# Attention ordered by whole pairs of heads in a fused attention and feed-forward kernel

## Chip, cores and metric

The kernel runs on one core of one Trainium2 chip. The metric is the device time of one execution in microseconds (us); smaller is better.

## What is computed

Two blocks follow each other. The attention has 4 batches, 8 heads, 768 positions and head size 64; its mask lets a query see only those keys whose six hashed sign bits equal its own. The feed-forward takes the 3072 rows of 512 values that the attention leaves.

```python
q_bits = (np.einsum('bhsd,dk->bhsk', q, proj) > 0)
k_bits = (np.einsum('bhsd,dk->bhsk', k, proj) > 0)
mask = q_bucket[:, :, :, None] == k_bucket[:, :, None, :]
scores = np.where(mask, scale * np.matmul(q, k.transpose(0, 1, 3, 2)), -1e9)
attn = np.exp(scores - np.max(scores, axis=-1, keepdims=True))
attn = attn / (np.sum(attn, axis=-1, keepdims=True) + 1e-09)
x = np.matmul(attn, v)             # then (B,H,S,D) -> (B*S, H*D)
h = x @ w_in                       # 512 -> 2048
sp = np.maximum(h, 0.0) + np.log1p(np.exp(-np.abs(h)))
out = (h * erf(sp)) @ w_out        # 2048 -> 512
```

## The kernel before

**Work of the attention.** Two heads are handled together as a pair, one on partitions 0 to 63 and one on 64 to 127; there are 16 pairs. A pair has two halves of 384 queries and, in each, two groups of three key chunks, so 4 groups n = 4i to 4i+3 of three blocks (n, c), 12 blocks. For a block TensorE computes scores of 128 keys by 384 queries for both heads (`score`, L548): first a bf16 product of the sign bits (`both`), which puts keys of another bucket far below zero, and onto it the float32 product of k and q. ScalarE takes the exponential into a block of `e_all` (`exponential`, L566). TensorE multiplies six blocks by v (`weigh`, L629, two groups per half) into `av`; ScalarE copies it out (`leave`, L688).

**Divisors.** VectorE adds the six blocks of a half (`sum_keys`, L617); TensorE sums over partitions with a matrix of ones (`divisor`, L664); ScalarE copies that out (`keep_divisor`, L677). Then the divisors go through DRAM to be spread over partitions: `spread`, `gather`, `invert`, `ungather`, `widen` (L707 to L742). `normalise` (L750) applies them and `send` stores x.

**Bits.** `bits_of` (L817) forms the projections of a later pair, ScalarE takes the sign (`sign_of`, L826), VectorE weighs them, and they go through DRAM into `both` by two steps on POOL's queue, `leave_bits` (L846) and `place_bits` (L855).

**Rooms.** Scores and bits share three double banks of PSUM (tag "big"); `av` has one bank, and z_ps takes the bank of `misc`. `e_all` is a ring of nine blocks. `x_sum` and `blocks[1]`, which the feed-forward uses later, hold the sums of the keys meanwhile.

**Weights.** Beside the attention 32 pieces of w_in and w_out are brought in as raw 64-bit numbers (`fetch_weights`, L454, on POOL's queue from the third on) and turned into float32: ScalarE `square_high` (L468) and `keep_normal` (L475), VectorE `move_bits`, `mask_bits`, `add_rest` (L482 to L530). `measure` (L649) takes sums of squares of q and k on ScalarE. `presum_weights` (L771) prepares sums and differences of blocks of w_in in `w_sum`, `presum_x` (L340) those of x; the feed-forward uses seven products P1 to P7 where the plain way needs eight, and likewise M1 to M7 for w_out.

**Order.** TensorE's order in the attention is written out by hand in the list `order`: score groups 2h+1 and 2h+2, at odd h the bits of a later pair, the divisor of the half before, and the two `weigh` of half h. All other engines follow a planner, `arrange`: each operation has an engine, an estimated cost, a rank, a list of what it comes after, and `late`, the time until others see its result; the planner always takes the operation that can start first, by rank among equals. What it emits is a fixed order per engine and per DMA queue; on the chip each engine then works through its own. The feed-forward is planned separately, so all of an engine's attention work stands ahead of its feed-forward work. The last pair's divisor is emitted in the feed-forward through `late`, as are its inversion and normalising.

## Time and profile before

| | us |
|---|---|
| median of 3 runs | 910.3 (910.22 to 911.51) |
| profiled execution | 910.96 |
| its span | 909.2 |
| feed-forward's first matmul starts | 321.51 |

The engines by stage, from the busy times of stretches of the trace (us, and the share of the 16 DMA engines):

| stretch | length | TensorE | VectorE | ScalarE | DMA |
|---|---|---|---|---|---|
| 50 to 89 | 39 | 37.63 | 35.44 | 30.68 | 0.59 |
| 128 to 167 | 39 | 39.00 | 37.43 | 31.65 | 0.64 |
| 245 to 284 | 39 | 39.00 | 36.96 | 31.64 | 0.60 |
| 321 to 360 | 39 | 39.00 | 30.60 | 27.13 | 0.31 |
| 360 to 900 | 540 | 540.00 | 347.28 | 290.62 | 0.19 |

In the profile a line such as L548 is a line of the kernel; "out<-in" are its tiles; "128*64" after a matmul's tiles is the part of the array that it uses, rows by columns. A float32 matmul shows as two records, and records of matmuls overlap, since they are pipelined. An idle time is followed by what ended it. PE is TensorE, PEld its loading of weights, DVE VectorE, ACT ScalarE, POOL GpSimd, SP SyncE.

### The profile page before, as it was taken

Reading aid. Unit: us, or ns where it says so; the run is one execution under the profiler, and the core shown is the slowest. Engines: PE = TensorE matmul, PEld = TensorE weight load, DVE = VectorE, ACT = ScalarE, POOL = GpSimd, SP = SyncE. Lnnn points to the kernel's source line nnn. Section 1 sums busy time; section 2 is a strip of 40 time slices with the busy share of each in tenths; the row PEclk is TensorE's granted clock in tenths of the full one; section 3 lists DMA queues with packets and bytes.
Section 4 is the critical chain, followed back from the end, with each engine's and each line's share of the span. In section 5 each row is a group of like instructions: output and inputs, shape, how many; then the busy total and the mean of one; then the engine's idle time right before and its main releaser. Section 6 shows DMA issues by size and latency. Waiting matters only on the chain.

```text
span 909.2 us, 12885 instructions
## 1 busy us (share of the span) xinstructions
PE 900.3 (99%) x5016; PEld 661.9 (73%) x5016; DVE 673.3 (74%) x863; ACT 571.9 (63%) x824; POOL 58.2 (6%) x95
## 2 busy tenths in 40 slices
PE   9999999999999999999999999999999999999997
PEld 5444444444444478888888888888888888888886
DVE  5989999989999969986566556756776556655653
ACT  6878887888887849755555545555655555545520
POOL 0211111111121000000000001000100000000000
PEclk9999999999999999999999999999999999999999
DMA  8455677656574231111122114211321023101321
GB/s 203 130 162 148 169 176 189 187 141 165 157 194 136 59 123 64 38 45 70 52 65 82 35 47 105 81 36 47 87 99 35 35 58 94 35 32 52 69 70 50
DMA packets 65013, 86.83 MB, mean 96 GB/s; under 512 B 34348, under 2 KB 47500, under 8 KB 64944
## 3 DMA queue, kind: packets, MB, share of 16 engines
q1 hardware_dynamic: 56384, 63.81, 24.6%
q0 software_dynamic: 8112, 21.66, 8.6%
q8 instruction: 41, 0.67, 0.3%
q10 hardware_dynamic: 448, 0.46, 0.2%
q14 instruction: 28, 0.23, 0.1%
HBM read 64.67 MB, written 17.30 MB: 90 GB/s over the span
## 4 chain that ended last, share of the span: by engine, by line
PE 92%; issue 1%; DMA 1%; ACT 0%; POOL 0%; DVE 0%; DVEq 0%; ACTq 0%; POOLq 0%
PE M L1317 32%; PE X L1204 28%; PE st L548 14%; PE av L629 12%; PE M L1204 3%; PE z_ps L664 1%; PE bits L817 1%; DMA raw<-in_w_in_dram 0%; POOL both L855 0%; ACT e_all L566 0%; ACT keep L468 0%; DMA bd<-sg 0%; DVE u L1352 0%; ACT x L688 0%; DVEq L1727 0%
## 5 line engine op out<-in xcount | busy, mean ns | idle before, releaser
L1244 DVE SCALAR_TENSOR_TENSOR e<-w,e 128x1024 f32<-128x1024 f32 x144 | 173.8, 1221 | 8.9 <-ACT w L1238 4.2
L566 ACT ACTIVATE e_all<-st 128x768 f32<-128x768 f32 x192 | 150.9, 813 | 11.9 <-PE st L548 11.5
L1238 ACT ACTIVATE w<-h,cq 128x1024 f32<-128x1024 f32 x144 | 155.6, 1137 | 0.2 <-DVE e L1244 0.2
L548 PE MATMUL st<-q,k 64*128 64x384 f32 x768 | 155.0, 483 | 0.0
L1226 DVE TENSOR_TENSOR h<-X,h 128x512 f32<-128x512 f32 x65 | 44.8, 689 | 146.0 <-PE X L1204 145.8
L1317 PE MATMUL M<-w_out_sb,h 128*128 128x256 f32 x576 | 141.5, 379 | 0.0
L629 PE MATMUL av<-e_all,v 128*64 128x385 f32 (+1 forms) x768 | 131.1, 490 | 0.0
L1204 PE MATMUL X<-x,w_in_sb 128*128 128x256 f32 x512 | 121.0, 379 | 0.0
L1317 PEld LDWEIGHTS M<-w_out_sb,h 128*128 128x128 f32 x576 | 109.4, 190 | 14.9
L1222 ACT COPY h<-X 128x512 f32<-128x512 f32 x85 | 49.3, 580 | 112.4 <-PE X L1204 112.3
L1234 ACT ACTIVATE e<-h,cq 128x1024 f32<-128x1024 f32 x48 | 55.2, 1150 | 82.7 <-DVE h L1226 82.7
L1204 PEld LDWEIGHTS X<-x,w_in_sb 128*128 128x128 f32 x512 | 97.3, 190 | 13.2
L629 PEld LDWEIGHTS av<-e_all,v 128*64 128x64 f32 x768 | 52.4, 136 | 67.2 <-issue 65.2
L1317 PE MATMUL M<-wt,S 128*128 128x256 f32 x384 | 95.6, 379 | 0.0
L548 PEld LDWEIGHTS st<-q,k 64*128 64x128 f32 x768 | 68.2, 188 | 34.9 <-issue 34.2
L1204 PE MATMUL X<-x_sum,w_sum 128*128 128x256 f32 x344 | 81.3, 379 | 0.0
L1317 PEld LDWEIGHTS M<-wt,S 128*128 128x128 f32 x384 | 73.0, 190 | 9.9
L1204 PEld LDWEIGHTS X<-x_sum,w_sum 128*128 128x128 f32 x344 | 65.4, 190 | 8.9
L548 PE MATMUL st<-both 64*128 64x384 bf16 x384 | 62.9, 324 | 1.6 <-ACT e_all L566 1.4
L1259 DVE TENSOR_TENSOR h<-h,e 128x1024 f32<-128x1024 f32 x48 | 58.0, 1221 | 3.7 <-ACT e L1255 3.6
L1255 ACT ACTIVATE e<-e 128x1024 f32<-128x1024 f32 x48 | 50.4, 1054 | 7.8 <-DVE e L1244 7.4
L548 PEld LDWEIGHTS <-both 64*128 64x128 bf16 x384 | 19.5, 94 | 43.1 <-issue 21.2
(126 smaller groups left out, 1073.4 us busy)
## 6 DMA issues: line engine op xcount, KB each, us to landing
wt<-wt SPq DMA_DIRECT2D x24, 768.0 KB, 4.2
raw<-in_w_out_dram POOLq DMA_DIRECT2D x16, 512.0 KB, 4.6
raw<-in_w_in_dram POOLq DMA_DIRECT2D x14, 512.0 KB, 4.3
v<-in_v_dram SPq DMA_DIRECT2D x32, 192.0 KB, 4.8
xs<-x SPq DMA_DIRECT2D x16, 384.0 KB, 3.1
q<-in_qkT_dram SPq DMA_DIRECT2D x30, 192.0 KB, 4.2
k<-in_qkT_dram SPq DMA_DIRECT2D x30, 192.0 KB, 4.4
r<-rd SPq DMA_DIRECT2D x30, 192.0 KB, 3.4
```

What stands on the lines that cost most here:

```text
L548: nc.tensor.matmul(out=st[:, ab, 0:HS], lhsT=d["k" + src][rows, keys], rhs=d["q" + src][rows, cols], start=(part == 0), stop=(part == 1),)
L566: nc.scalar.activation(out=e[:, :, 0:HS], in_=st[:, :, 0:HS], func=AF.Exp, scale=scale)
L629: nc.tensor.matmul(out=d["av"][rows, 0:w], lhsT=d["v"][:, g * GC + c, rows], rhs=e[:, ab, 0:w], start=(g == 0 and c == 0), stop=(g == 1 an ...
L1204: nc.tensor.matmul(out=d[where][:, u, :], lhsT=a[:, kc, f : f + P], rhs=b[:, kc, :], start=(first and u == 0 and kc == 0), stop=(last and ...
L1222: nc.scalar.copy(out=quarter(p, q), in_=st[p][where])
L1226: nc.vector.tensor_tensor(out=h, in0=st[p][where], in1=h, op=ALU.add)
L1234: nc.scalar.activation(out=s, in_=unit(p, v), func=AF.Sigmoid, bias=cq[:, n : n + 1])
L1238: nc.scalar.activation(out=q, in_=unit(p, v), func=AF.Sigmoid, scale=GATE_S[j][0], bias=cq[:, j : j + 1])
L1244: nc.vector.scalar_tensor_tensor(out=s, in0=st[p].pop(("q", v, j)), scalar=GATE_S[j][2], in1=s, op0=ALU.add, op1=ALU.mult,)
L1255: nc.scalar.activation(out=s, in_=s, func=AF.Tanh, scale=GATE_LEAD)
L1259: nc.vector.tensor_tensor(out=h, in0=h, in1=st[p].pop(("s", v)), op=ALU.mult)
L1317: nc.tensor.matmul(out=banks[name][:, sub, :], lhsT=a[:, u, sub * P : (sub + 1) * P], rhs=b[:, u, :], start=(c == 0 and k == 0), stop=(c = ...
```

## The change

- TensorE's order is by whole pairs: the 12 score blocks of a pair, then `weigh` of all four groups (24 products with v, one for each block and head, which are 48 records in the profile), then the bits of pair i+2 and the divisor of pair i-1. Pair 0 has bits 1 ahead of its products with v, and the last pair has the divisor there.
- One divisor step covers both halves of a pair. It writes into the second bank of the double bank that holds the bits, so the two share one of the three slots of the scores, which is free when both have been copied out.
- The halves' products with v have two banks: the old one and that of `misc`.
- Each half of a pair has six blocks of its own for its exponentials: `e_even`, and `e_odd`, which lies in the room of `w_sum`. `area` holds w_sum, blocks[0], x_sum and blocks[1] in this order. The last half of all uses tiles of the load pool.
- The sums of keys are formed with five wide additions per pair, in two rooms that alternate by pair.
- As `w_sum` is occupied, `presum_weights` 0 to 3 run in the last pair and 4 to 7 in the feed-forward (`late` 3 to 6, ahead of the third product's P5, P6, P7 and P3). Loading the first tile of x and preparing it come later too.
- There are three rooms for raw pieces instead of two, and two each for `keep` and `top`; a piece is asked for every 1.9 groups instead of 2.

```diff
-    w_sum = const.tile([P, 3, 2, FH], F32, name="w_sum")
+    AW, AX_, AB = 6 * FH, 6 * TH, NK * T
+    area = const.tile([P, AW + AX_ + 2 * AB], F32, name="area")
+    w_sum = area[:, 0:AW].rearrange("p (n k c) -> p n k c", n=3, k=2)
+    x_last = const.tile([P, HS], F32, name="x_last")
...
-    x_sum = const.tile([P, 3, 2, TH], F32, name="x_sum")
-    for n in range(2):
-        blocks.append(const.tile([P, NK, T], F32, name=f"x{n}"))
+    x_sum = area[:, AW + AB : AW + AB + AX_].rearrange("p (n k c) -> p n k c", n=3, k=2)
+    for at in (AW, AW + AB + AX_):
+        blocks.append(area[:, at : at + AB].rearrange("p (k t) -> p k t", k=NK))
...
-            tc.tile_pool(name="rawp", bufs=2) as rawp,
+            tc.tile_pool(name="rawp", bufs=3) as rawp,
...
-            NE = 3 * GC
-            e_all = ep.tile([P, NE, 2, HS + 1], F32, name="e_all")
-            nc.vector.memset(e_all[:, :, :, HS : HS + 1], 1.0)
+            NE = 2 * GC
+            e_even = ep.tile([P, NE, 2, HS + 1], F32, name="e_even")
+            nc.vector.memset(e_even[:, :, :, HS : HS + 1], 1.0)
+            e_odd = area[:, 0 : NE * S].rearrange("p (n a c) -> p n a c", n=NE, a=2)
+            e_last = {}
...
-                for t in (x_sum[:, :, :, :], blocks[1][:, :, :].rearrange("p k (a t) -> p k a t", a=2))
+                area[:, at : at + 4 * S].rearrange("p (h n a c) -> p h n a c", h=2, n=2, a=2)
+                for at in (AW + AB, NE * S)
             ]
+            last_sums = blocks[1][:, :, :].rearrange("p k t -> p (k t)")[:, 0 : 2 * S].rearrange(
...
-                keep = cvt.tile([P, WP], I32, name="keep", tag="keep")
+                keep = cvt.tile([P, WP], I32, name="keep", tag="keep", bufs=2)
...
-                return e_all[:, (n * GC + c) % NE, :, :]
+                if n == NS - 2 or n == NS - 1:
+                    what, m = "qkv"[c], n - (NS - 2)
+                    if (m, c) not in e_last:
+                        shape = [P, NC, P] if what == "v" else [P, S]
+                        room = load.tile(shape, F32, name=what, tag=what)
+                        if what == "v":
+                            room = room.rearrange("p c d -> p (c d)")
+                        e_last[m, c] = room[:, 0:S].rearrange("p (a c) -> p a c", a=2)
+                    return e_last[m, c]
+                return (e_odd if n // 2 % 2 else e_even)[:, n % 2 * GC + c, :, :]
...
+            def sum_steps(i):
+                n = 4 * i
+                if i < NPAIR - 1:
                     return [
-                        ((0, 1, 2, 3), (0, 2), (2, 2), 2),
-                        ((4, 5), "s2", (4, 2), 2),
-                        ((), "s0", "s1", 0),
+                        ((0, 0, 4), (0, 1, 2, 3)),
+                        ((0, 4, 2), (4, 5)),
+                        ((1, 0, 4), (6, 7, 8, 9)),
+                        ((1, 4, 2), (10, 11)),
+                        (None, ()),
                     ]
                 return [
-                    ((0, 1, 3, 4), (0, 2), (3, 2), 2),
-                    ((2,), "s0", (2, 1), 0),
-                    ((5,), "s1", (5, 1), 1),
-                    ((), "s0", "s1", 0),
-                ]
-            def last_sum(h):
-                return len(sum_steps(h)) - 1 if h >= 0 else 0
-            def sum_keys(h, k):
-                i, half = divmod(h, 2)
+                    ((0, 0, 4), (0, 1, 2, 3)),
+                    ((0, 4, 2), (4, 5)),
+                    ((0, 6, 0), ()),
+                ] + [((1, k, 1), (6, 7) if k == 1 else (6 + k,)) for k in range(1, 6)]
...
-                    d["av"] = psum_v.tile([P, 512], F32, name="av", tag="av")
+                    d["av", half] = bank("av") if half else psum_v.tile([P, 512], F32, name="av", tag="av")
...
+                if i == NPAIR - 1:
+                    z = bank("z_ps")[:, 0:HS]
+                else:
+                    room = pairs[i + 3]["bits"] if i + 3 < NPAIR else big("z_ps")
+                    z = room[:, 1, 0:HS]
+                d["z_ps"] = z
+                for half in range(2):
+                    for n in range(4):
+                        ab, part = divmod(n, 2)
+                        nc.tensor.matmul(
+                            out=z[n * QR : (n + 1) * QR, half * HS // 2 : (half + 1) * HS // 2],
+                            lhsT=ones[:, 0:QR],
+                            rhs=d["sum"][:, half, ab, part * HS // 2 : (part + 1) * HS // 2],
+                            start=True,
+                            stop=True,
+                        )
...
+            def keep_divisor(i):
                 d = pairs[i]
-                if half == 0:
-                    d["z"] = home(i, "z")
-                nc.scalar.copy(
-                    out=d["z"][:, half * HS // 2 : (half + 1) * HS // 2], in_=d.pop("z_ps")
-                )
+                d["z"] = home(i, "z")
+                nc.scalar.copy(out=d["z"], in_=d.pop("z_ps"))
...
-            order = [("score", 0)]
-            for h in range(NH):
-                order += [("score", n) for n in (2 * h + 1, 2 * h + 2) if n < NS]
-                if h == 0:
+            order = []
+            PACE = 19
+            for i in range(NPAIR):
+                order += [("score", 4 * i + k) for k in range(4)]
+                if i == 0:
                     order.append(("bits", 1))
-                if h % 2 and (h + 3) // 2 < NPAIR:
-                    order.append(("bits", (h + 3) // 2))
-                if h >= 1:
-                    order.append(("divisor", h - 1))
-                order += [("weigh", 2 * h), ("weigh", 2 * h + 1)]
+                if i == NPAIR - 1:
+                    order.append(("divisor", i - 1))
+                order += [("weigh", 4 * i + k) for k in range(4)]
+                if i + 2 < NPAIR:
+                    order.append(("bits", i + 2))
+                if 0 < i < NPAIR - 1:
+                    order.append(("divisor", i - 1))
             slots = []
             for what, n in order:
+                free = slots[-3] if len(slots) >= 3 else ()
                 if what == "score":
                     i = n // 4
                     after = (("double_first",) if i == 1 else ("place_bits", i),)
                     for c in range(GC):
-                        free = (slots[-3],) if len(slots) >= 3 else ()
+                        free = slots[-3] if len(slots) >= 3 else ()
                         pe(score, (n, c), 0.82 if n or c == 2 else 0.17, after + free)
-                        slots.append(("exponential", n, c))
+                        slots.append((("exponential", n, c),))
                 elif what == "bits":
-                    pe(bits_of, (n,), 0.92 if n > 1 else 1.44, (("start_pair", n), slots[-3]))
-                    slots.append(("sign_of", n) if n > 1 else ("place_first",))
+                    pe(bits_of, (n,), 0.80 if n > 1 else 1.44, (("start_pair", n),) + free)
+                    slots.append((("sign_of", n),) if n > 1 else (("place_first",),))
                 elif what == "divisor":
-                    pe(divisor, (n,), 0.42, (("sum_keys", n, last_sum(n)), ("keep_divisor", n - 1)))
+                    if n + 3 < NPAIR:
+                        free = ()
+                        slots[-1] += (("keep_divisor", n),)
+                    else:
+                        slots.append((("keep_divisor", n),))
+                    pe(divisor, (n,), 0.72, (("sum_keys", n, last_sum(n)),) + free)
                 else:
                     h = n // 2
                     after = (("exponential", n, GC - 1),)
                     if n % 2 == 0:
-                        after += (("leave", h - 1), ("leave_plain", (h - 1) // 2))
-                    pe(weigh, (n,), 2.02, after)
+                        after += (("leave", h - 2), ("leave_plain", (h - 2) // 2))
+                    pe(weigh, (n,), 2.0, after)
...
+                    after = (("score", n, c), ("weigh", n - 4)) + sums_after.get((n - 4, c), ())
+                    if n >= NS - 2:
+                        after += tuple(
+                            ("measure", i, m, half)
+                            for i in (NPAIR - 3, NPAIR - 2)
+                            for m in range(2)
+                            for half in range(2)
+                        )
+                    op(exponential, (n, c), "ACT", 0.735, (0, n, c), after)
...
-                    (("start_pair", 1), ("fetch_weights", n - 1), ("add_rest", n - 2), ("exponential", max(2 * n - 2, 0), 1)),
+                    (("start_pair", 1), ("fetch_weights", n - 1), ("add_rest", n - 3), ("exponential", max(PACE * n // 10 - 2, 0), 1)),
...
-                op(square_high, (n,), "ACT", 0.68, (1, n, 0), (fetched, ("mask_bits", n - 1)))
+                op(square_high, (n,), "ACT", 0.68, (1, n, 0), (fetched, ("mask_bits", n - 2)))
...
-            for k in range(8):
+            for k in range(4):
...
+                        ("weigh", NS - 5),
+                        ("sum_keys", NPAIR - 2, last_sum(NPAIR - 2)),
+                    )
+                    + ((("sum_keys", NPAIR - 1, 2),) if k % 4 == 3 else ()),
+                )
+            op(load_x, (0,), "SP", 1.1, (1, 0), (("send", JP - 1), ("divisor", NPAIR - 3)), late=4.0)
             for k in range(4):
-                op(presum_x, (0, k), "DVE", 0.62, (2, 31, 8 + k), (("load_x", 0), ("presum_x", 0, k - 1), ("divisor", NH - 3)))
+                op(presum_x, (0, k), "DVE", 0.62, (2, 31, 8 + k), (("load_x", 0), ("presum_x", 0, k - 1), ("divisor", NPAIR - 2)))
...
+            else:
+                presum_weights(k + 1)
...
+                for k in range(3, 7):
+                    op(("late", k), "DVE", 1.2, (2, 1, -7 + k), late, (k,), after=(("late", k - 1),) if k > 3 else ())
+                for each in ops:
+                    if each.name in (("P5", 2), ("P6", 2), ("P7", 2), ("P3", 2)):
+                        each.after += (("late", 6),)
```

Not shown: renamed arguments, the planner's estimated costs, ranks and dependencies of the sums, and the last pair's x, which is kept, normalised and sent in two halves.

## The prediction

> **What bounds the kernel now.** The page's first part comes first: who is busy, and in how much of the span.
>
> ```profile
> PE 900.3 (99%) x5016; PEld 661.9 (73%) x5016; DVE 673.3 (74%) x863; ACT 571.9 (63%) x824; POOL 58.2 (6%) x95
> ```
>
> TensorE works in all but 9 us of 909.2. So the stage that is changed can gain from less TensorE time per pair, or from a stall that goes; it loses where a new wait reaches TensorE. The second view is TensorE's own waits up to 400 us:
>
> ```profile
> PE st L548 <- ACT e_all L566: 1.4, 1, 1.4
> PE warm L779 <- DVE ones L247: 1.0, 1, 1.0
> PE st L548 <- ACT both L384: 0.3, 1, 0.3
> ```
>
> Two of these lie in the start-up. The 1.4 us is one event at 62.3 us, looked at below. As nothing else is idle, I read the third view, TensorE's timeline over one pair (two half-pairs), start and length in front:
>
> ```profile
> 158.91 0.34 PE L548 MATMUL st<-both 64*128 64x384 bf16 x2
> 159.08 0.81 PE L548 MATMUL st<-q,k 64*128 64x384 f32 x4
> ...
> 162.96 0.33 PE L548 MATMUL st<-both 64*128 64x384 bf16 x2
> 163.12 0.81 PE L548 MATMUL st<-q,k 64*128 64x384 f32 x4
> 163.86 0.52 PE L817 MATMUL bits<-q,proj_q 128*32 128x384 f32 x2
> ...
> 164.53 0.51 PE L664 MATMUL z_ps<-x_sum,ones 128*32 128x192 f32 x8
> 164.97 4.09 PE L629 MATMUL av<-e_all,v 128*64 128x384 f32 x24
> 168.99 0.34 PE L548 MATMUL st<-both 64*128 64x384 bf16 x2
> ...
> 173.94 0.53 PE L664 MATMUL z_ps<-x,ones 128*32 128x192 f32 x8
> 174.40 4.10 PE L629 MATMUL av<-e_all,v 128*64 128x385 f32 x24
> 178.44 0.34 PE L548 MATMUL st<-both 64*128 64x384 bf16 x2
> ```
>
> The lengths overlap, so I use starts. A pair takes 178.44 - 158.91 = 19.53 us. A score block takes (163.12 - 159.08)/5 = 0.808 us: three passes of two row tiles, one in bf16 (0.16) and one float32 product that counts as two (0.323 each, (0.808 - 0.16)/2).
>
> Six blocks are 4.85 us, but bits begin 4.95 us after the first: 0.10 us is lost where the score run ends. The 24 records of products with v are 12 passes of two column tiles, 12 x 0.323 = 3.88 us; the next run begins after 4.02 to 4.04: 0.15 lost. A divisor is two passes of 192 columns, 2 x 0.162 = 0.32 us, and v's products begin after 0.44 to 0.46: 0.125 lost. Bits to divisor is 0.67 us, two passes of 0.323 and 0.02 lost. So each hand-over between kinds of matmul costs 0.10 to 0.15 us, except between two of one shape.
>
> **What the Trainium skill says.** "TensorEngine Tiling (Array Packing)", Key Properties: a change of the tiling mode, not just of the tile, drains the engine. The trace agrees: the losses are where 64*128, 128*32 and 128*64 meet, and bits to divisor, both 128*32, is nearly free. "TensorE: Matmul & The Clock Gate", Back-to-back issue gap: N/2.4 + 2.5 ns, 162 ns for 384 columns; the bf16 pass (0.16) and half a float32 product (0.323/2) agree. The same page's table of specifications calls the other engines' queues strictly first in, first out; the 1.4 us stall is such a case. "DMA: Bandwidth & Descriptors", Issuing engines are not separate DMA queues: transfers of all issuers interleave on the same 16 engines; below, a small one took 6.4 us beside loads.
>
> **The change, part by part.**
>
> Order on TensorE (the main gain). Run ends before: 32 score runs (0.10), 32 runs of products with v (0.15), 31 divisors (0.125): 3.2 + 4.8 + 3.9 = 11.9 us. After: 16, 16, and 16 ends of slots with a divisor or bits (pair 0 has bits alone, pairs 1 to 14 one slot, pair 15 a divisor): 1.6 + 2.4 + 2.0 = 6.0. The streams are the same: 192 score blocks, 768 records with v, 15 products for bits. Gain 5.9 us, about 0.39 per whole pair (19.14). Against it: the divisor left for the feed-forward stage is now a whole pair's, four passes instead of two, +0.32. Net -5.6. Two hand-overs are not in the trace: products with v to bits, and divisor to scores, some 14 each. At least nothing (bits 128*64 to v at the start followed at the stream's pitch, 16.15 to 16.47), at most twice the dearest seen, 0.3: against the 0.15 and 0.125 that I take this is -3.9 to +4.5 us if both went to the same end; I keep +-2 for the range, since all switches seen lie within 0.05 of each other.
>
> Bits and divisor in one PSUM slot. Scores use three slots; the third block of a pair now waits for the slot that sign_of and keep_divisor must empty. From the last product with v (T): bits from T+0.15, divisor T+0.82 to T+1.47, first block T+1.6, third T+3.2. ACT: leave 0.48, sign 0.46, then the copy, now 384 wide, 0.48 (the leave's row): done near T+2.2. Spare 1.0 us. Nothing; if one measure (0.64) stands before them, still nothing. The second av bank only loosens.
>
> Runs of 12 against ScalarE. After the stall ACT did four exponentials in 2.92 us, so saturated pitch is (2.92 - 0.81)/3 = 0.703, against 0.808 for a block: it gains 0.105 per block. A squaring or a piece's first step put into a run costs it 0.50 to 0.57 (163.07 to 163.57; 152.82 to 153.39), and before TensorE waits it may be late by 0.58 (first exponential ends 160.75, fourth block starts 161.33). One such op fits, a second after five or six blocks. ACT's sum per pair: 12 x 0.703, two leaves 0.96, sign 0.46, copy 0.48, four measures 2.56, 2.1 pieces at 1.38: 15.8 of 19.1 us. So nothing.
>
> VectorE. Five wide steps of 1.79 (165.37 to 167.16) are 8.95 per pair against about 9.1; pieces at 2.1 per pair instead of 2 add 0.38; four preparations of W_in (4.9 us) leave the stage. It stays at 96% (37.43 of 39 us), but what waits for it has more room: a block is overwritten 19 us after its exponential instead of 14. Nothing.
>
> The end of the stage. In the last pair's 19 us VectorE has three wide and five narrow sums (9.3), four preparations (4.9), the four of x (2.75) and a normalise (1.0): about 18. The first to be missed is P6, 3.5 us into the feed-forward (325.07 before), which needs the x sums; I put these some 5 us before it. The other four preparations, 4.9 us, fall between 324 and 342, where VectorE idled 7 us; they are due at the third product (343.4). Nothing; without that cover, up to 3 us. Loading x later: one whole pair remains for 4 us of transfer. Nothing. The two sends and two normalises of pair 15: a late transfer, needed a tile later.
>
> The stall at 62.3 us. POOL's, ACT's and TensorE's timelines there:
>
> ```profile
> 48.72 0.55 POOL L846 DMA_DIRECT2D bd<-sg  x1 [5.14 <-DVE sg L836]
> 55.77 1.15 POOL L855 DMA_DIRECT2D both<-bd  x2 [6.50 <-issue]
> 56.91 1.14 POOL L454 DMA_DIRECT2D raw<-in_w_in_dram  x2
> ```
>
> ```profile
> 61.11 0.69 ACT L468 ACTIVATE keep<-raw 128x512 f32<-128x512 f32 x1 [4.75 <-DMA raw<-in_w_in_dram]
> 61.83 0.72 ACT L475 ACTIVATE keep<-keep,tiny 128x512 int32<-128x512 f32 x1
> 62.46 0.46 ACT L688 COPY x<-av 128x384 f32<-128x384 f32 x1
> 62.82 2.92 ACT L566 ACTIVATE e_all<-st 128x768 f32<-128x768 f32 x4
> ```
>
> ```profile
> 63.68 0.34 PE L548 MATMUL st<-both 64*128 64x384 bf16 x2 [1.37 <-ACT e_all L566]
> ```
>
> The bits' transfer took 6.4 us because the next pair's q, k, v (issued 47.24 to 50.37) were in flight; the fetch of a raw piece was queued on POOL behind the placing of the bits; the piece landed at 61.03; ACT's squaring waited in order, and leave and exponentials behind it. With three raw rooms and two keep and top rooms a fetch may be asked for earlier, so this event should go (-1.37). But bits now fall right at the pair's end, where the next load becomes free to start: the same meeting can come in any pair. Each costs up to 1.4. I take 1.1 for them, under one event; bounds 0 and 14 events.
>
> Sum, on the profiled execution (910.96; span 909.2 and 1.8 around it): -5.6 - 1.4 + 1.1 = -5.9, 905.1. The median of the runs is 0.66 below that execution: 904.4.
>
> **The rivals.**
>
> Slower: the bits' traffic delays the pieces in nearly every pair. Place: POOL's queue, then ACT's squaring in front of exponentials. Price 1.4 per pair; the gain of 7.0 is gone from five events on, and 13 of them give 910.3 - 7.0 + 18 = 921; nine, which I take for its time, 916. For it: loads and bits start together. Against: only one of 14 placings did this before; a fetch has a median landing of 4.3 to 4.6 us and 7.0 are planned.
>
> ScalarE in the runs of 12: a third op in a run, or one that carries lateness over, costs 0.5 in each of 14 pairs: +7, 910. For it: spare of 0.58 against 0.57. Against: the pitch, and that ops are put in only when ACT has caught up.
>
> Dear hand-overs: the two new ones cost 0.25 each, +3, 907.5. For it: never seen. Against: every drain seen.
>
> **How the numbers follow.** Forecast 0.70, 904.4, own range 902 to 907.5 (hand-overs +-2, no stall or two). Dear hand-overs 0.06, ScalarE 0.09, slower rival 0.15. The range leaves out the slower rival and a little of the others: 901.8 to 909.8. A measurement of this kernel tells 0.2% (1.8 us) from no change. Faster, below 908.5: 0.70 + 0.06 + a bit of ScalarE's, 0.77; within, 0.07; slower, above 912.1, 0.16.
>
> **What would show it.** Right: a pair on TensorE's timeline of 19.1 to 19.2 us; scores 12 x 0.808; 48 records with v, then bits, divisor, scores with 0.10 to 0.15 at each change; the feed-forward beginning near 315 instead of 321.5, and as long as before. Wrong: waits of TensorE for exponentials in several pairs, with ACT idle for a raw piece before them (slower rival) or without idle time (ScalarE's); a gap at P6 or at the third product (preparations late); a pair near 19.5 without waits (hand-overs).

## The result, and the profile after

The changed kernel takes 916.05 us (median of 5 runs, 914.37 to 916.87) against 910.8 us (910.22 to 911.94) for the kernel before on the same chip: a ratio of 1.0053 (of the means, as all ratios here), 95% interval 1.0039 to 1.0068. It is slower by about 5 us, where 6 us less had been forecast. The profiled execution is 916.7 us, its span 914.9.

The page's line of busy times for the changed kernel:

```profile
PE 897.7 (98%) x5016; PEld 673.0 (74%) x5016; DVE 668.7 (73%) x837; ACT 562.9 (62%) x808; POOL 58.2 (6%) x95
```

TensorE is busy 2.6 us less than before, yet it is now idle for 17 us of its span instead of 9. What it waited for up to 420 us (total, times, longest, in us):

```profile
PE M L1241 <- DVE h L1263: 5.3, 1, 5.3
PE M L1241 <- ACT h L1259: 2.1, 1, 2.1
PE st L554 <- ACT z L691: 1.7, 1, 1.7
...
PE st L554 <- ACT e_even L581: 0.2, 1, 0.2
```

The two largest are not in the attention (L554 is `score`) but in the feed-forward (L1241 is its product), and neither was there before. They add up to 7.4 us, most of the new idle time. First the attention. TensorE's timeline over one whole pair of the changed kernel, start and length in front:

```profile
161.34 0.34 PE L554 MATMUL st<-both 64*128 64x384 bf16 x2
...
171.13 4.10 PE L639 MATMUL av<-e_even,v 128*64 128x385 f32 x24
175.07 4.04 PE L639 MATMUL av<-area,v 128*64 128x384 f32 x24
179.04 0.52 PE L838 MATMUL bits<-q,proj_q 128*32 128x384 f32 x2
...
179.71 0.83 PE L680 MATMUL bits<-area,ones 128*32 128x192 f32 x16
180.47 0.34 PE L554 MATMUL st<-both 64*128 64x384 bf16 x2
```

A pair takes 180.47 - 161.34 = 19.13 us; 19.14 had been worked out. The feed-forward's first matmul starts at 315.53, 5.98 us earlier than before. From that start to the start of its last product it then takes 906.38 - 315.53 = 590.85 us, where the kernel before took 901.11 - 321.51 = 579.60: 11.25 us are lost behind the place that the change was meant for. With 0.43 us more in the tail, -5.98 + 11.25 + 0.43 gives the 5.7 by which the span grew. TensorE's timeline there, before and then after:

```profile
310.00 0.53 PE L664 MATMUL z_ps<-x,ones 128*32 128x192 f32 x8
...
321.51 3.72 PE L1204 MATMUL M<-x,w_in_sb 128*128 128x256 f32 x16
...
332.64 1.89 PE L1204 MATMUL M<-x_sum,w_in_sb 128*128 128x256 f32 x8
334.36 3.62 PE L1204 MATMUL M<-x,w_in_sb 128*128 128x256 f32 x16
337.82 3.62 PE L1204 MATMUL M<-x_sum,w_sum 128*128 128x256 f32 x16
...
901.11 1.89 PE L1317 MATMUL M<-w_out_sb,S 128*128 128x256 f32 x8
```

```profile
306.84 0.86 PE L680 MATMUL z_ps<-area,ones 128*32 128x192 f32 x16
...
315.53 3.72 PE L1241 MATMUL M<-area,w_in_sb 128*128 128x256 f32 x16
321.35 3.72 PE L1241 MATMUL M<-area 128*128 128x256 f32 x16 [2.10 <-ACT h L1259]
325.00 0.86 PE L680 MATMUL z_ps<-area,ones 128*32 128x192 f32 x16
...
334.77 7.99 PE L1241 MATMUL M<-area,w_in_sb 128*128 128x256 f32 x24 [5.26 <-DVE h L1263]
342.60 3.62 PE L1241 MATMUL M<-area 128*128 128x256 f32 x16
...
906.38 1.89 PE L1354 MATMUL M<-w_out_sb,S 128*128 128x256 f32 x8
```

Two idle times, 2.10 and 5.26. The 24 records after the second take 342.60 - 334.77 = 7.83 us; before, 24 such records took 5.18 (332.64 to 337.82). The difference, 2.65 us, is the clock. The view of stretches shows it in the first number after the busy times (stretch, length, then busy times of PE, PEld, DVE, ACT, POOL, then the granted clock as a share of full speed, the DMA share and GB/s):

```profile
334.00:343.00 9.00, 8.23 (x26) 6.87 (x27) 2.96 (x8) 3.67 (x5) 0.00 (x0) 0.67 0.37 132
343.00:365.00 22.00, 21.93 (x103) 18.42 (x103) 19.63 (x27) 19.24 (x23) 0.00 (x0) 1.00 0.20 66
```

So the 11.25 us are 2.10 + 5.26 + 2.65 + 0.33 (the late divisor of a whole pair, 0.79 instead of 0.46) and a rest of 0.9, about half of it (0.49) behind 342.60 and not followed further.

**Behind the first wait** is ScalarE's copy of the first product out of PSUM:

```profile
320.71 0.59 ACT L1259 COPY h<-M 128x512 f32<-128x512 f32 x1 [4.59 <-DVE area L627]
```

It writes `h`, and waits for VectorE's sums of keys (L627): the `h` tiles of the feed-forward lie in the rooms of the load pool, and there the change put the exponentials of the last half, which these sums read. The last of the sums ends at 320.48.

**Behind the second wait** is VectorE's own queue. Its timeline after the last sum (L766 is `normalise`, L1326 prepares w_out, L792 is `presum_weights`, L1263 the awaited addition):

```profile
319.52 0.96 DVE L627 TENSOR_TENSOR area<-area,v 128x768 f32<-128x768 f32 x1
324.10 1.02 DVE L766 SCALAR_TENSOR_TENSOR x<-x,ev,r 128x768 f32<-128x768 f32 x1 [3.61 <-DMA r<-rd]
325.03 0.68 DVE L1326 TENSOR_TENSOR wt<-w_out_sb 128x512 f32<-128x512 f32 x1
...
327.56 1.22 DVE L792 TENSOR_TENSOR area<-w_in_sb 128x1024 f32<-128x1024 f32 x1
...
334.03 0.68 DVE L1263 TENSOR_TENSOR h<-M,h 128x512 f32<-128x512 f32 x1
```

The division of pair 14 stands in front of all of VectorE's feed-forward work and waits 3.61 us for its divisors; behind it come six preparations of w_out and the four of w_in that the change moved here, and only then the addition that TensorE needs. The divisors are late, and SP's queue shows a part of the reason (L755 is `widen`, L720 `spread`):

```profile
311.32 1.25 SPq L755 DMA_DIRECT2D r<-rd  x2
312.67 0.56 SPq L720 DMA_DIRECT2D zd<-z  x1
...
319.89 1.25 SPq L755 DMA_DIRECT2D r<-rd  x2
```

The divisor of pair 14 was on TensorE at 306.84 and copied out from 307.76 to 308.24, but its spreading is queued behind the widening of pair 13 and goes out at 312.67, 4.4 us later; after another 11.4 us the widened divisors have landed, at 324.1. In the kernel before, the divisors of the last half but one had 11.5 us before the feed-forward began (310.00 to 321.51); now there are 8.7. There the spreading went out at 310.95, as soon as ScalarE had copied, and `normalise` waited 0.24 us:

```profile
323.40 1.02 DVE L750 SCALAR_TENSOR_TENSOR x<-x,ev,r 128x768 f32<-128x768 f32 x1 [0.24 <-DMA r<-rd]
```

So the way from the divisor's product to `normalise` was 13.4 us before (310.00 to 323.40) and is 17.3 now (306.84 to 324.10): the divisors come 0.7 us later than before, while VectorE is ready for them 2.7 us earlier, and that makes the new wait.

**The one stall inside the attention**, 1.7 us near 203, begins on POOL's queue and goes through ScalarE. POOL's timeline, then ScalarE's:

```profile
191.52 1.16 POOL L876 DMA_DIRECT2D both<-bd  x2 [4.44 <-DMA bd<-sg]
192.67 1.66 POOL L460 DMA_DIRECT2D raw<-in_w_out_dram  x3
```

```profile
196.60 0.69 ACT L474 ACTIVATE keep<-raw 128x512 f32<-128x512 f32 x1 [4.83 <-DMA raw<-in_w_out_dram]
...
202.56 0.47 ACT L691 COPY z<-bits 128x384 f32<-128x384 f32 x1
```

ScalarE waits 4.83 us for a raw piece, and a pair that has three pieces follows; the copy of the divisor (L691), which empties the slot that the third score block needs, ends at 203.03. ScalarE waits for raw pieces ten times in the stage now, 27.5 us in all (before: once, 4.8), but TensorE felt it in this one pair only. On POOL's queue, from 54.7 us on, the fetches of a pair go out right behind the placing of the bits, as they do here at 192.67.

### The profile page after: what moved, and what is told of

Its sections match the earlier page's. It is cut to its first block, busy times and chain, and to the rows that moved or that the text cites. A ratio compares the mean times of both kernels' runs of the same rounds, so it can differ in the third digit from the quotient of the medians.

```text
span 914.9 us, 12791 instructions
## 1 busy us (share of the span) xinstructions
PE 897.7 (98%) x5016; PEld 673.0 (74%) x5016; DVE 668.7 (73%) x837; ACT 562.9 (62%) x808; POOL 58.2 (6%) x95
## 3 DMA queue, kind: packets, MB, share of 16 engines
q0 software_dynamic: 8112, 21.66, 8.5%
## 4 chain that ended last, share of the span: by engine, by line
PE 87%; DMA 5%; DVE 5%; ACT 1%; issue 1%; SPq 0%; POOL 0%; DVEq 0%; ACTq 0%; POOLq 0%
PE M L1354 32%; PE X L1241 28%; PE st L554 13%; PE av L639 9%; PE M L1241 2%; DMA r<-rd 2%; DMA rd<-zc 1%; PE bits L838 1%; DMA zd<-z 1%; DVE area L792 1%; DVE area L627 1%; PE bits L680 1%; DMA zc<-zd 1%; DVE x L766 1%; PE warm L800 0%
## 5 line engine op out<-in xcount | busy, mean ns | idle before, releaser
L1241 PE MATMUL X<-area,w_in_sb 128*128 128x256 f32 x680 | 160.7, 379 | 0.0
L554 PE MATMUL st<-q,k 64*128 64x384 f32 x768 | 155.1, 483 | 0.0
L1263 DVE TENSOR_TENSOR h<-X,h 128x512 f32<-128x512 f32 x65 | 44.8, 689 | 145.0 <-PE X L1241 144.9
L1241 PEld LDWEIGHTS X<-area,w_in_sb 128*128 128x128 f32 x680 | 129.3, 190 | 17.5
L1241 PE MATMUL X<-area 128*128 128x256 f32 x520 | 123.0, 379 | 0.1
L1241 PEld LDWEIGHTS X<-area 128*128 128x128 f32 x520 | 98.8, 190 | 13.8 <-DVE h L1263 0.5
L554 PEld LDWEIGHTS st<-q,k 64*128 64x128 f32 x768 | 69.0, 187 | 29.9 <-issue 27.4
L627 DVE TENSOR_TENSOR area<-area 128x1536 f32<-128x1536 f32 (+1 forms) x46 | 79.3, 1724 | 3.4 <-ACT area L581 1.4
L581 ACT ACTIVATE e_even<-st 128x768 f32<-128x768 f32 x96 | 70.3, 823 | 0.7 <-PE st L554 0.7
L581 ACT ACTIVATE area<-st 128x768 f32<-128x768 f32 x90 | 67.9, 813 | 0.0
L554 PE MATMUL st<-both 64*128 64x384 bf16 x384 | 63.7, 324 | 2.2 <-ACT z L691 1.7
L639 PE MATMUL av<-e_even,v 128*64 128x385 f32 x384 | 65.6, 490 | 0.0
L639 PE MATMUL av<-area,v 128*64 128x384 f32 x360 | 60.6, 486 | 0.0
```

The source lines that it names most:

```text
L554: nc.tensor.matmul(out=st[:, ab, 0:HS], lhsT=d["k" + src][rows, keys], rhs=d["q" + src][rows, cols], start=(part == 0), stop=(part == 1),)
L581: nc.scalar.activation(out=e[:, :, 0:HS], in_=st[:, :, 0:HS], func=AF.Exp, scale=scale)
L627: nc.vector.tensor_tensor(out=into, in0=one, in1=two, op=ALU.add)
L639: nc.tensor.matmul(out=d["av", half][rows, 0:w], lhsT=d["v"][:, g * GC + c, rows], rhs=e[:, ab, 0:w], start=(g == 0 and c == 0), stop=(g = ...
L1241: nc.tensor.matmul(out=d[where][:, u, :], lhsT=a[:, kc, f : f + P], rhs=b[:, kc, :], start=(first and u == 0 and kc == 0), stop=(last and ...
L1263: nc.vector.tensor_tensor(out=h, in0=st[p][where], in1=h, op=ALU.add)
```

## The experiments

Each row stands against runs of the kernel before on the same chip; the changed kernel itself is 1.0053. Waits are read from the one profiled execution of each kernel, which can be a fast or a slow one of its runs.

| experiment | us, median (range, runs) | ratio to before | 95% interval |
|---|---|---|---|
| last half's sums first | 918.94 (916.41 to 921.35, 6) | 1.0084 | 1.0066 to 1.0101 |
| pair 14 not divided | 910.93 (910.18 to 912.31, 13) | 1.0003 | 0.9995 to 1.0012 |
| four preparations left out | 910.27 (908.17 to 912.01, 13) | 0.9991 | 0.9983 to 1.0000 |
| four preparations later | 912.06 (910.91 to 915.52, 16) | 1.0020 | 1.0011 to 1.0030 |
| divisors earlier | 913.75 (911.77 to 915.16, 8) | 1.0028 | 1.0018 to 1.0038 |
| three of these together | 909.90 (907.57 to 912.40, 14) | 0.9992 | 0.9982 to 1.0002 |
| preparations on GpSimd | 915.33 (915.02 to 917.83, 5) | 1.0055 | 1.0042 to 1.0068 |
| fetches planned as later | 919.29 (914.53 to 921.04, 6) | 1.0080 | 1.0059 to 1.0101 |
| pieces evenly spaced | 910.31 (906.76 to 913.44, 14) | 0.9993 | 0.9980 to 1.0006 |
| VectorE's costs as measured | 911.93 (908.09 to 916.60, 22) | 1.0015 | 1.0005 to 1.0025 |
| rooms in another order | 913.16 (912.60 to 918.56, 9) | 1.0040 | 1.0024 to 1.0055 |
| the same, pieces on SP's queue | 907.47 (907.18 to 908.40, 5) | 0.9962 | 0.9949 to 0.9976 |

A stall in the attention differs from run to run and hides in these times. So it helps to look at the feed-forward alone, from the start of its first product to the start of its last, in the profiled executions: 579.6 us before, 590.9 in the changed kernel, 591.8 with the sums first, 581.7 without the division, 584.4 without the preparations, 585.3 with them later, 586.6 with earlier divisors, 581.5 with three of these together.

**The first wait alone: the last half's sums ahead of the preparation of x.**

```diff
-                    rank = (3 if i == NPAIR - 1 and k > 2 else 1, 4 * i + 1 + k // 2, k)
+                    rank = (1, 4 * i + 1 + k // 2, k)
```

> The five narrow sums of the last half come ahead of the preparation of x on VectorE. Theory (VectorE's in-order queue at the start of the feed-forward is what TensorE waits for, above all the normalising of pair 14, which itself waits for its widened divisors until 324.1 us): the first wait (2.1 us, for rooms of h that the sums still read) goes, but TensorE only comes earlier to the second, which grows by the same: 916 us, within 1. Rival (the waits are independent, each with its own price): 2.1 us less, 914.

TensorE's timeline, waits of the feed-forward only:

```profile
322.90 3.69 PE L1241 MATMUL M<-area 128*128 128x256 f32 x16 [0.27 <-DVE area L343]
...
338.55 8.36 PE L1241 MATMUL M<-area,w_in_sb 128*128 128x256 f32 x24 [7.52 <-DVE h L1263]
```

The first wait falls to 0.27 and the second grew from 5.26 to 7.52: removing one wait in front of another only moves the time, as expected. The time itself was not 916 but 918.9. In the profiled execution (920.9, one of the slower) the attention had 4.2 us of waits instead of 1.9, and the feed-forward began at 318.90, 3.4 us later; its own length grew by only 1.0. This edit didn't aim at the attention, and why it got longer stays open.

**The second wait, two causes taken away one at a time.** First `normalise` returns for pair 14, then the four late preparations are left out.

```diff
+                if i == NPAIR - 2:
+                    return
```

> Pair 14 is stored without its division: the normalising that waits 3.6 us for a transfer at the head of VectorE's feed-forward work is left out, its transfers stay. Theory (a wait in VectorE's queue): VectorE is 4.6 us earlier at its feed-forward work, the second wait of TensorE falls from 5.3 to about 0.7, the clock is not lowered (2.65): 909. Rival (VectorE has simply too much work there, the wait is filled anyway): only the 1.0 us of the operation is gained, 915.

```diff
-                presum_weights(k + 1)
+                pass
```

> The four preparations of the input weights in the feed-forward are left out, 4.9 us of VectorE work; the products of the third block on use what lies there. Theory (queue): all four stand ahead of the addition that TensorE waits for, so the second wait falls by 4.6 and the lowered clock goes: 909. Rival (only the wait for the divisors counts, the preparations lie in idle time as I predicted): no change, 916.

TensorE's timelines at the second wait, without the division and then without the preparations:

```profile
332.40 5.45 PE L1243 MATMUL M<-area,w_in_sb 128*128 128x256 f32 x24 [0.62 <-DVE h L1265]
```

```profile
331.80 5.45 PE L1241 MATMUL M<-area,w_in_sb 128*128 128x256 f32 x24 [0.67 <-DVE h L1263]
```

Either is enough: the second wait is 0.62 us without the division and 0.67 without the preparations, which is 5.26 less the 4.63 us of waiting and dividing, or about less the 4.9 us of preparing. The times are 910.9 and 910.3, some 5 to 6 below the changed kernel and level with before. They stand 1 to 2 us above what was expected, with waits of 3.3 and 2.7 us in the attention; behind the one of 3.3 us four score blocks took 5.98 us instead of 3.23, another 2.7 us, at a clock of 0.50.

The feed-forward without the division began at 319.76, 4.2 us later than in the changed kernel, so VectorE had more time before it, which fits that the first wait is gone there too. It doesn't explain the second: from the end of the last sum to that of the awaited addition VectorE took 14.2 us in the changed kernel (320.48 to 334.71) and 9.6 here (322.75 to 332.35), less by those 4.63.

**The same work in another order.** The four preparations come after the addition that TensorE waits for.

```diff
-  after=(("late", k - 1),) if k > 3 else ())
+  after=((("late", k - 1),) if k > 3 else (("complete", 0, 3),)))
```

> Same work, but the four preparations come after the second addition of the first product set (complete for P7). Theory (order in the queue, not the amount): as without them, 909. Rival (amount of VectorE work in the first 35 us): the wait only moves to the third product, which needs the preparations, 914 or more.

TensorE's timeline:

```profile
322.44 5.41 PE L1241 MATMUL M<-area 128*128 128x256 f32 x16 [2.17 <-ACT h L1259]
...
332.82 5.45 PE L1241 MATMUL M<-area,w_in_sb 128*128 128x256 f32 x24 [0.54 <-DVE h L1263]
```

The wait falls to 0.54, nothing new waits at the third set of products, which needs them, and 3 us (by the ratios) to 4 us (by the medians) come back. So most of what the four preparations cost was their place. The time is 912.1, between the expected 909 and the rival's 914 and 1.8 above that of the kernel without them. In the profiled execution the first wait, 2.17, was followed by a lowered clock, which cost 1.69 us (16 records in 5.41 instead of 3.72); in the one without preparations it wasn't.

**The divisors earlier.** That of pair 13 goes ahead of the products with v of pair 14, that of pair 14 into the middle of the last 12 score blocks.

```diff
+                order += [("score", 4 * i + k) for k in range(2)]
+                if i == NPAIR - 1:
+                    order.append(("divisor", i - 1))
+                order += [("score", 4 * i + k) for k in range(2, 4)]
...
-                if i == NPAIR - 1:
+                if i == NPAIR - 2:
                     order.append(("divisor", i - 1))
...
-                if 0 < i < NPAIR - 1:
+                if 0 < i < NPAIR - 2:
```

> Only TensorE's order at the end is changed: the divisor of pair 13 comes ahead of pair 14's products with v, that of pair 14 after six of the last pair's twelve score blocks. It costs one more hand-over pair (0.25 us). Theory (what hurts is that the chain of five transfers behind the last divisors has 9 us before the feed-forward instead of 11.5, and that VectorE's queue stands still for it): the wait for the widened divisors at the head of the feed-forward goes or falls under 1 us, and the time is as without the division, 911. Rival (VectorE's work alone fills this time): 915 or 916.

The second wait goes entirely; the first becomes 3.93. The last sum, for which `h` waits, ends 6.8 us after the feed-forward's start (324.91 against 318.13) instead of 5.0. The work ahead of it is the same, the division of pair 14 stands behind it (at 324.83); but VectorE, which had no gap there before, now stood idle for 1.42 us until pair 13's divisors came to be inverted at 305.48. The time, 913.75, is 2.3 below the changed kernel, and lies between the expected 911 and the rival's 915.

**All three together.**

> Earlier divisors, sums of the last half ahead of the preparation of x, and the four preparations of weights after the second addition of the first product set, together. Theory: all waits of TensorE at the start of the feed-forward fall under 1 us in sum and the clock stays up: 916 - 10 = 906, faster than the kernel before (911). Rival (amount of VectorE work): no better than the preparations moved alone, 912.

The feed-forward's waits are 0.42 and 0.18 us, and the time is 909.9: the loss is given back, but the expected gain over before isn't there. What is left in the profile is 2.5 us of waits in the attention, the longest 1.95 for the copy of a divisor, and runs that differ by 5 us. The profiled execution (908.02) is one of the fastest, so it doesn't show what the slower ones lost.

**The preparations on GpSimd** (with the last half's sums first and the earlier divisors; the planner is told the engine and 2.6 us for each).

```diff
-                nc.vector.tensor_tensor(out=out_, in0=one_, in1=two_, op=op_)
+                engine = nc.vector if k < 4 else nc.gpsimd
+                engine.tensor_tensor(out=out_, in0=one_, in1=two_, op=op_)
```

> As the three changes, but the four preparations of weights in the feed-forward run on GpSimd, which is idle there, instead of later on VectorE. If VectorE's amount of work still counts, this is faster than the three changes by up to 2 us; if only the order counts, it is the same within 1 us. If GpSimd is slower than 4 us an operation, the third product waits for it and it is slower.

POOL's timeline and then VectorE's:

```profile
296.64 3.83 POOL L793 TENSOR_TENSOR area<-w_in_sb 128x1024 f32<-128x1024 f32 x1 [5.40 <-PE av L639]
```

```profile
299.35 1.93 DVE L766 SCALAR_TENSOR_TENSOR x<-x,ev,r 128x768 f32<-128x768 f32 x1 [1.03 <-DMA r<-rd]
301.20 2.58 DVE L488 TENSOR_SCALAR top<-raw 128x512 int32<-128x512 int32 x1
303.82 2.74 DVE L496 SCALAR_TENSOR_TENSOR top<-raw,top 128x512 int32<-128x512 int32 x1
```

GpSimd took three of the four not in the feed-forward but in the last pair, as soon as their inputs were free, 11 to 20 us before the feed-forward began (317.00). VectorE's operations of 1.02, 0.42 and 0.69 us took 1.93, 2.58 and 2.74 beside them, and a sum of 0.96 took 2.91 beside the fourth: 7.1 us more in all. TensorE waited 7.48 us for the preparation of x, where it waited 0.42 with the three edits: again 7.1. So none of the three outcomes named above came: GpSimd's operations took 2.5 to 3.8 us, and the loss came from VectorE, which they slowed where it was already late.

**Why the attention still stalls.** Three tries on the raw pieces and the planner, all on top of the three edits: `late` of a fetch 10 instead of 7; then a piece every two groups; then that with VectorE's estimated costs raised to the measured ones.

```diff
-                    late=7.0,
+                    late=10.0,
```

> The three changes, and the planner reckons 10 us instead of 7 for a raw piece to land, so ScalarE's squarings stand later in its order. Theory (the wait of 1.7 to 4 us for a score slot in the middle of the attention comes from a piece that lands late behind the bits' transfer on GpSimd's queue, with leave, sign and the divisor's copy queued behind its squaring): this wait goes, 2 us less than the three changes. Rival (the slot is late for another reason, the fetch's own order): no change.

```diff
- ("exponential", max(PACE * n // 10 - 2, 0), 1)
+ ("exponential", max(2 * n - 6, 0), 1)
```

> The three changes, and a raw piece is asked for every 2 groups, from six groups earlier, instead of every 1.9: no pair gets three. Theory (the wait of 1.7 to 2.5 us in the middle of the attention is in the one pair that gets three pieces: ScalarE stands before its three squarings for late pieces, and the copy of the divisor that empties a score slot is queued behind them): it goes, and with it most of the spread of the three changes: 907.5, faster than the kernel before. Rival (late pieces do it wherever they fall, as two did at 62 us in the kernel before): as the three changes, 910, with waits in other pairs.

```diff
- "DVE", 1.05, ...   "DVE", 1.1, ...   "DVE", 1.3, ...   1.72 if wide else 0.92
+ "DVE", 1.2, ...    "DVE", 1.2, ...   "DVE", 1.35, ...  1.8 if wide else 1.0
```

> As even_pace, and the planner reckons with VectorE's durations as the traces show them (sums 1.8 and 1.0 instead of 1.72 and 0.92, the steps of a piece 1.2, 1.2, 1.35 instead of 1.05, 1.1, 1.3). If VectorE's lateness against the plan at the pair's end (the weighing of the bits comes 5 us after their products) makes the late pieces, ScalarE's waits for raw pieces fall well under the 20 to 28 us of the runs so far and the time is the same or lower by up to 1 us. If the transfers themselves make them, no change.

Planning a later landing did harm: ScalarE's waits for raw pieces rose to 33.6 us, TensorE's in the attention to 7.3, and the feed-forward waited 3.5 for the preparation of x. Even spacing left ScalarE waiting 24.4 us; the pair that stalled was another one (1.3 us at 183.57). With truer costs ScalarE waited 21.7, and the median was 1.6 higher; VectorE's waits for divisors were 19.6 against 13.4, but the first stands in one of the slowest executions (914.7) and the second in one of the fastest (908.1). None of the three brought ScalarE's waits for pieces under 20 us.

**The rooms, and then the queue.** The first kernel has the later preparations, the earlier divisors and the even spacing; the sums stay where the change put them, and the pools of the feed-forward are opened in another order so that `h` doesn't lie on the last half's exponentials. The second differs from it only in who fetches the raw pieces, for the chip and for the planner.

```diff
-            tc.tile_pool(name="hp", bufs=8) as hp,
-            tc.tile_pool(name="sums", bufs=1) as sums,
+            tc.tile_pool(name="outp", bufs=1) as outp,
             tc.tile_pool(name="wtp", bufs=2) as wtp,
+            tc.tile_pool(name="sums", bufs=1) as sums,
+            tc.tile_pool(name="hp", bufs=8) as hp,
             tc.tile_pool(name="work", bufs=1) as work,
-            tc.tile_pool(name="outp", bufs=1) as outp,
```

> The changed kernel with four edits: the last four preparations of W_in behind P3, the divisors of pairs 13 and 14 earlier in TensorE's order, the pieces spaced evenly, and the rooms of the feed-forward placed in another order, so that the h tiles no longer lie on the blocks of exponentials that the last half's sums read. The sums keep the place that the change gave them, behind the sums of x. Theory (the first wait of the feed-forward comes from the rooms, the second from the order on VectorE): both waits go without moving the sums, TensorE's waits in the feed-forward fall below 0.7 us in all, and the time is 906 to 908, faster than before. Rival (VectorE simply has too much to do in the last pair, and whatever stands last there is waited for): a wait of 1 to 3 us shows at another place of the first tile, and the time is 909 to 912, as that of the three changes together.

```diff
-                queue = nc.sync if n < 2 else nc.gpsimd
+                queue = nc.sync
...
-                    "SP" if n < 2 else "POOL",
+                    "SP",
```

> The same kernel with the raw pieces fetched on SP's queue instead of POOL's. Theory (late pieces come from POOL's queue, where a fetch stands behind the placing of the bits): ScalarE's waits for raw pieces fall from 22 us to below 8, TensorE's waits in the attention fall below 0.5 us, the spread of the runs narrows, and the time is 1 to 2 us below the same kernel with POOL's queue. Rival (it is the transfers that meet on the DMA engines, or SP's queue has waits of its own, for divisors and stores of x): ScalarE's waits for raw pieces stay above 15 us, and the time is the same or longer.

TensorE's timeline at the second run of products (P6 and P5), with the rooms and then also SP's queue:

```profile
323.94 6.17 PE L1244 MATMUL M<-area 128*128 128x256 f32 x16 [6.75 <-ACT h L1262]
```

```profile
319.94 3.72 PE L1244 MATMUL M<-area 128*128 128x256 f32 x16 [1.60 <-ACT h L1262]
```

ScalarE's waits up to 325 us, again first with POOL's queue:

```profile
ACT keep L474 <- DMA raw<-in_w_out_dram: 23.1, 8, 4.6
...
ACT keep L474 <- DMA raw<-in_w_in_dram: 1.4, 1, 1.4
```

```profile
ACT keep L474 <- DMA raw<-in_w_in_dram: 1.2, 1, 1.2
```

How the pieces go out in one pair, on POOL's queue and then on SP's:

```profile
170.87 1.16 POOL L876 DMA_DIRECT2D both<-bd  x2 [4.30 <-PE st L554]
172.03 1.14 POOL L460 DMA_DIRECT2D raw<-in_w_out_dram  x2
```

```profile
164.04 0.43 SPq L460 DMA_DIRECT2D raw<-in_w_out_dram  x1
...
169.16 0.42 SPq L460 DMA_DIRECT2D raw<-in_w_out_dram  x1
```

The rooms with POOL's queue failed, at 913.2 instead of 906 to 908: the sums no longer hold `h`, but something else does, for 6.75 us. With SP's queue the profile names it: the store of x (pair 14's, issued at 316.43, ended 2.9 us later), whose room `h` now takes. For the other kernel the same reading fits (a store issued at 320.44, the copy into `h` at 323.31), though its trace names an operation of VectorE; it was not tried apart. So the rival of that run, whatever stands last is waited for, was right in kind, though its wait of 1 to 3 us at another place came as 6.75 at the same one.

SP's queue bore out its theory beyond what was expected: ScalarE's waits for raw pieces fall from 24.5 to 1.2 us, VectorE's for divisors from 14.4 to 1.8, its last sum ends 4 us earlier (315.47 instead of 319.48), and the time is 5.7 us lower. TensorE's waits in the attention were expected below 0.5, but there was one of 1.2, where the other profile had none. At 907.47 us this is the only version whose interval lies below the kernel before. Three things changed at once: the pieces no longer stand behind the placing of the bits, the planner gave SP's other transfers another order, and POOL's queue appears in the profile as a software one, SP's as a hardware one (the software queue's 21.66 MB became 5.92). These weren't tried apart, nor was this edit on the changed kernel alone.

## Why the prediction was wrong

**The order on TensorE** (-5.6): right. The pair is 19.13, the feed-forward begins at 315.53 where "near 315" was written. The two hand-overs not seen before, products with v to bits and divisor to scores, cost about 0.15 and 0.11 (180.47 - 179.71 = 0.76, four passes of 0.162 and 0.11), as taken. The late divisor's +0.32 is 0.33.

**Bits and divisor in one slot** ("Spare 1.0 us. Nothing"): no wait came of it but in one pair. There the copy ended 5.0 us after the last product with v (203.03 against 198.0) instead of 2.2, since late pieces had put ScalarE behind.

**Runs of 12 against ScalarE**: right, 0.2 us in all.

**VectorE in the stage**: the load was over-estimated and the reason for ease was right. It was busy 32.95 of 39 us (128 to 167) instead of 96%, partly as it waited for divisors (16.3 us up to 325); TensorE never waited for it there.

**The stall at 62.3**: it went. For new ones 1.1 was set down; 1.9 came. The slower rival's mechanism is there in ten waits, so its premise was right and its price, 1.4 per event on TensorE, was not. That the rival's time, 916, is the one measured is chance: it stood for nine waits of TensorE in the attention, and the loss lies in the feed-forward. Late pieces may reach the time in another way: with the fetches on SP's queue, the end of the stage is earlier on VectorE.

**The end of the stage** is the step that failed: "Nothing; without that cover, up to 3 us". Four things in it.
- The last pair's VectorE work was put at about 18 us in 19. From 297.81 to 320.48 it was 22.7 us without a break: the last piece (3.6) had slipped into it, a second `normalise` (1.0) and the reciprocals (0.8) were not counted.
- `normalise` was costed at its 1.0 us of work and not at its wait. The earlier start that was counted as the gain took 2.8 us from the divisors' way through DRAM, that way itself grew by 3.9 us, mostly in SP's queue, and 3.61 us of waiting came of it, in front of everything else on VectorE.
- The preparations were to fall into VectorE's idle time between 324 and 342. That time was idle only because VectorE, in order, waited for products; the four stood ahead of the addition that lets P4 go on. Putting them behind it gave 3 to 4 us back.
- What a tile's room had held before was looked at inside the attention, and not for `h`. That gave the first wait, 2.10, and its cost was never set down. Nor was that of the clock, 2.65. A gap at P6, which opens the second run of products, had been named as a sign of late preparations; the gap came there, but x's preparation had ended at 314.49, 4.6 us before P6 could start (319.09), as reckoned.

The named cover was the right thing to ask about; but "up to 3 us" reckoned with uncovered work alone, while the loss was wait, work and clock together, 11.25. The experiments show the second wait's two causes and the first wait's room. That late pieces push VectorE's work into the last pair fits the run with SP's queue, but isn't shown, as order and kind of queue changed with it. Open remains why runs of several of these kernels with the pieces on POOL's queue differ by 4 to 8 us.

## What to carry to other kernels

When a stage gets shorter, go through what the next stage first needs and count each chain's time to it anew, with its transfers and its place in each in-order queue: a gain of 6 us in front can come out as a wait of 7 behind. An engine's idle time is room for moved work only behind the operation that others await. And a queue shared by a small transfer that must wait and a large one that others need is worth trying to split before costs in a planner are tuned: here the tuning gave nothing and the other queue 5.7 us.

## What the runs showed of the hardware

- After 5.26 us of idle time TensorE's clock was 0.67 over the stretch of 9 us from 334 on. The Trainium skill, "TensorE: Matmul & The Clock Gate", What's actually happening, has the rate halved after an idle window of about 3.4 us; that fits. But 2.17 us sufficed with the preparations later (16 records took 5.41 us instead of 3.72) and 3.26 us without the division (0.50 from 206 to 210), while 2.10 us in the changed kernel, 2.77 without the preparations and even 3.31 with fetches planned as later (1.00 from 225 to 231) cost nothing. So below some 3.5 us the length of the idle time alone didn't decide.
- Beside GpSimd's operations VectorE's took 1.9 to 6 times as long. The skill's "SBUF — State Buffer", Who interferes with whom, says that a VectorE instruction with two inputs in SBUF contends with a GpSimd instruction that reads it; the trace agrees, with 0.69 grown to 2.74, and shows it for one with a single input too (L488, 0.42 to 2.58). That is a kind which the page says can enter modes with two ports, and those contend as well; which mode it ran in no run shows.
